# Handing over the next steps' preparation behind both halves of a cell visit, in an mLSTM cell followed by a leaky-ReLU feed-forward

## The chip, the cores and the metric

One core of a Trainium2 chip runs the whole program. The metric is device time in microseconds (us); lower is better. A core has five engines with instruction streams of their own: TensorE (PE, matmuls, its weight loads shown as PEld), VectorE (DVE), ScalarE (ACT), GpSimd (POOL) and SyncE (SP). Nearly all DMAs of this kernel are issued by SP, one after the other.

## The reference

An mLSTM cell runs over 768 time steps for 4 batch entries and 8 heads of 40 values, and its output, laid out as 3072 tokens of 320 values, goes through a feed-forward with 2048 hidden values:

```python
for t in range(S):
    m_new = np.maximum(f_gate[:, :, t] + m, i_gate[:, :, t])
    f_stab = np.exp(f_gate[:, :, t] + m - m_new)
    i_stab = np.exp(i_gate[:, :, t] - m_new)
    m = m_new
    C = f_stab * C + i_stab * np.einsum('bhd,bhe->bhde', vt, kt)
    n = f_stab * n + i_stab * kt
    h_tilde = np.einsum('bhde,bhe->bhd', C, qt)
    denom = np.maximum(np.abs(np.einsum('bhd,bhd->bh', n, qt)[:, :, None]), 1.0)
    y[:, :, t] = sigmoid(o_gate[:, :, t]) * h_tilde / denom
x = y.transpose(0, 2, 1, 3).reshape(B * S, H * D)
h = x @ w_in
out = np.maximum(0.01 * h, h) @ w_out
```

All data are float32 in the profile.

## The kernel before

The sequence is cut into six chunks of 128 tokens. A **step** `s` is one batch entry in one chunk: `s = 4*c + b`, 24 in all. The recurrence is computed in its chunked form: inside a step two halves of 64 tokens are handled with matmuls, and a state `S` is carried from half to half.

**Chunk loop.** For `c` from 1 to 6 the program works through the feed-forward of chunk `c-1` (the list `ffs`, built by `ff_units`) and, between its units, through the cell of chunk `c` (the list `cells`). From `c = 2` on `ffs` has 30 units. Units 0 to 15 are `firsts`: pairs of matmul runs with `w_in` (line 759, tile `ph`, input `xT`), then the leaky ReLU on ACT (line 767) into `acts`. Units 16 to 29 are `fast_units`, the multiplication with `w_out` done with seven products on sums and differences of quarters (Strassen's scheme in Winograd's form), each for `n = 0, 1`: `p1`, `p2`, `p6`, `p7`, `p4`, `p5`, `p3` in this order (matmuls on line 835, tile `po`). The quarter `(n, 0, 1)` of `acts` is read by `p2`, is then overwritten by the difference `s4`, and `s4` is read by `p3`, the last product.

**Cell visits.** `pairs` names the unit behind which cell work is emitted: behind unit 2 `u_parts` for steps 0 and 1 of the chunk, behind unit 6 `u_mix` for both, behind unit 14 `u_parts` for steps 2 and 3, and behind unit 19 (the second `p2`) `u_gates` for the next chunk, then `u_mix` for steps 2 and 3. `u_parts` makes the scores and the first half of the state. `u_mix` multiplies (line 695, tile `pT`), transposes on DVE (`hb`, 702), makes denominators (633 to 635), the gated product `xb` (706), the state sum (596), a POOL product (709), a second DVE transpose into `x` (713), and stores `x` to a scratch `x_dr` in DRAM with four DMAs (716).

**Preparation.** `ahead(s)` prepares step `s`: `prep_kq` on DVE (two transposes, line 505, and two products, line 511), a POOL product for the state (`state_next`, 592), a POOL product for `vu` (478), and ten loads on SP for the step after the next: four of k and four of q (line 398) and two of `ea` (line 421), which wait until `prep_kq` has read the buffers that they overwrite. `u_mix(s)` is followed by `ahead(s + 2)`.

**Gathers.** `gather_x(s)` brings `x_dr[s]` back as `xT`, laid out for `w_in`, with four DMAs (line 730). `xT` has one buffer for a whole chunk, so the gathers start behind unit 15. For the second `u_mix` visit of a chunk (behind unit 19) they follow the visit at once, eight DMAs for two steps. The next chunk's unit 0 reads their result. Behind them come, per step, four loads of the output gate (398), one of k (356), four of v (359) and two broadcasts `w` (413): 22 loads for a visit, called "feed loads" below.

**What sets the order.** PE, DVE, ACT and POOL run in the order in which the program emits (`tc.manual_schedule`). SP is not in that list: its order is made by the framework's planner, which takes the earliest instruction of the program that it holds to be ready. PSUM tiles of the cell share four banks (`psc`), those of the feed-forward four others (`psf`).

Of the kernel before, what the change touches and what calls it, by code (L numbers as in the profile page):

```python
# [13 lines left out]
ALU = mybir.AluOpType  # L14
# [4 lines left out]
def kernel(  # L19
# [26 lines left out]
    nc = tc.nc  # L46
# [44 lines left out]
    def load_fi(c):  # L91
        t = fi[c] = wk.tile([BH, 2, P], F32, name="fi")
        eng = nc.scalar if c < 3 else nc.sync
        eng.dma_start(t[:, 0, :], f_all[:, ts(c, P)])
        eng.dma_start(t[:, 1, :], i_all[:, ts(c, P)])
# [206 lines left out]
    def gates_exp(c):  # L302
        bu, a, na = bus[c]
        if c == 0:
            nc.scalar.activation(bu[:, 1, :], bu[:, 0, :], AF.Exp, bias=a[:BH, P - 1 :], scale=1.0)
            return
        for u in range(2):
            at = ts(u, SL)
            last = SL * (u + 1) - 1
            nc.scalar.activation(bu[:, 2, at], a[:, at], AF.Exp, bias=na[:] if u else 0.0, scale=1.0)  # L310
            nc.scalar.activation(bu[:, 1, at], bu[:, 0, at], AF.Exp, bias=a[:, last : last + 1], scale=1.0)
        if c > 0:
            nc.sync.dma_start(a_dr[c, 0].rearrange("u n t -> n u t"), a[:].rearrange("n (u t) -> n u t", u=2))
            if c > 1:
                nc.sync.dma_start(a_dr[c, 1].rearrange("u n t -> n u t"), bu[:, 2, :].rearrange("n (u t) -> n u t", u=2))
            if 1 < c < NB - 2:
                load_fi(c + 2)
# [498 lines left out]
    def quarter(n, i, k):  # L816

        return acts[:, k * KH : (k + 1) * KH, ts(2 * i + n, P)]
# [5 lines left out]
    def fast_units(g):  # L824


        t1 = low_w[:, :, NH:]
        t2, t3, t4 = t_at
        y = [[None, None], [None, None]]
        t = p1_at  # L830

        def product(n, left, right):
            bank = psf.tile([P, NH], F32, name="po", tag="mm")
            for f in range(KH):
                nc.tensor.matmul(bank[:], lhsT=left[:, f, :], rhs=right[:, f, :], start=f == 0, stop=f == KH - 1)  # L835
            return bank[:]

        def half(n, i, d):
            if y[i][n] is None:
                if i == 0:  # L840
                    y[i][n] = wk.tile([P, Dm], F32, name="y")[:]
                else:
                    y[i][n] = wk.tile([P, H, D1], F32, name="hn")[:].rearrange("p h d -> p (h d)")[:, :Dm]
            return y[i][n][:, ts(d, NH)]

        def send(n, i):
            b = 2 * i + n
            nc.sync.dma_start(out[b * S + g * P : b * S + (g + 1) * P, :], y[i][n])

        def p1(n):  # L850
            got = product(n, quarter(n, 0, 0), low_w[:, :, :NH])
            s1 = quarter(n, 1, 0)
            nc.vector.tensor_tensor(s1, s1, quarter(n, 1, 1), op=ALU.add)
            nc.scalar.copy(t[n], got)
            if n == 1:
                for m in range(2):
                    s2 = quarter(m, 0, 0)
                    nc.vector.tensor_tensor(s2, quarter(m, 1, 0), s2, op=ALU.subtract)

        def p2(n):  # L860
            got = product(n, quarter(n, 0, 1), high_w[:, :, :NH])
            nc.vector.tensor_tensor(half(n, 0, 0), t[n], got, op=ALU.add)
            s4 = quarter(n, 0, 1)
            nc.vector.tensor_tensor(s4, s4, quarter(n, 0, 0), op=ALU.subtract)

        def p6(n):
            got = product(n, quarter(n, 0, 0), t2)
            u2 = half(n, 0, 1)
            nc.scalar.copy(u2, got)
            nc.gpsimd.tensor_tensor(u2, u2, t[n], op=ALU.add)  # L870

        def p7(n):
            got = product(n, s3_at[:, n], t3)
            u3 = half(n, 1, 1)
            nc.scalar.copy(u3, got)
            nc.gpsimd.tensor_tensor(u3, u3, half(n, 0, 1), op=ALU.add)

        def p4(n):
            got = product(n, quarter(n, 1, 1), t4)
            c21 = half(n, 1, 0)  # L880
            nc.scalar.copy(c21, got)
            nc.gpsimd.tensor_tensor(c21, c21, half(n, 1, 1), op=ALU.add)

        def p5(n):
            got = product(n, quarter(n, 1, 0), t1)
            for i in (1, 0):
                nc.vector.tensor_tensor(half(n, i, 1), half(n, i, 1), got, op=ALU.add)  # L887
            send(n, 1)

        def p3(n):  # L890
            got = product(n, quarter(n, 0, 1), high_w[:, :, NH:])
            nc.vector.tensor_tensor(half(n, 0, 1), half(n, 0, 1), got, op=ALU.add)
            send(n, 0)

        return [lambda p=p, n=n: p(n) for p in (p1, p2, p6, p7, p4, p5, p3) for n in range(2)]

    def u_gates(c):
# [43 lines left out]
    def feed(s):  # L941
        load(s)
        spread(s)
# [78 lines left out]
    with tc.manual_schedule(engines={E.PE, E.DVE, E.Activation, E.Pool}):  # L1022
        ffs = first_chunk()
        for s in (B, B + 1):
            feed(s)
            for i in range(1, 3):
                load_late(s, i)
            if s == B:
                load_weights(3)
        for n in range(3):  # L1030
            load_weights(QN + n)
        for s in (B + 2, B + 3):
            feed(s)


        ffs = ffs[2:]
        fetch = {4: (3, 4), 8: (5, 6), 15: (7,)}
        place = (2, 5, 7, 10, 12, 15, 16, 18, 21, 22, 24, 26, 28)
        late = {}
        masks = {0: (2, 3), 12: (4, 5)}  # L1040
        pairs = (2, 2, 6, 6, 14, 14, 19, 19, 19)
        now = (None for n in range(2, QN + NF // 2) for _ in narrow_weights(n))
        for c in range(1, NB + 1):
            if c > 1:
                ffs = ff_units(c - 1)
            cells = cell_units(c) if c < NB else []
            n_ff, n_c = len(ffs), len(cells)
            done = fed = 0
            waiting = []
            for i in range(n_ff):  # L1050
                if c == 1:
                    run(now, 2 if i < 10 else 3 if i < 14 else 4)
                    for n in fetch.get(i, ()):
                        load_weights(QN + n)
                    if i == 0:
                        prep_mask(B)
                        ahead(B)
                        load_fi(3)
                for s, steps in lazy.items():
                    if s in late and late[s] > 0:  # L1060
                        late[s] -= 1
                    else:
                        run(steps, 3)
                for n in masks.get(i, ()) if 1 < c < NB else ():
                    if c * B + n < NS:
                        prep_mask(c * B + n)
                ffs[i]()
                if c + 1 < NB:
                    if i == (1 if c == 1 else 0):
                        gates(c + 1)  # L1070
                    if c == 2 and i == 0:
                        mixed_weights()
                    if i == (3 if c == 1 else 2):
                        gates_exp(c + 1)
                upto = min(n_c, sum(p <= i for p in (place if c == 1 else pairs)))
                while done < upto:
                    fn, s = cells[done]
                    fn(s)
                    done += 1
                    if fn is u_mix:  # L1080
                        waiting.append(s)
                    if fn is u_plain and s < 2 * B - 1 or fn is u_parts and s == 2 * B - 1:
                        ahead(s + 1)
                    elif fn is u_mix:
                        ahead(s + 2)
                    elif fn is u_plain:
                        prep_mask(s + 2)
                        ahead(s + 2)
                if i >= NF - 1:
                    for s in waiting:  # L1090
                        gather_x(s)
                    waiting.clear()
                while fed < done:
                    fn, s = cells[fed]
                    fed += 1
                    if fn in (u_mix, u_plain):
                        load_late(s + NR, 2)
                        if s + NL < NS:
                            feed(s + NL)
# [31 lines left out]
```

## Time and profile before

| | us |
|---|---|
| median of 3 runs | 513.13 (512.97 to 515.71) |
| the profiled execution | 516.18 |
| its span | 514.4 |
| PE busy in it | 496.0 |
| DVE busy | 305.8 |
| ACT busy | 171.3 |
| POOL busy | 130.6 |

The span is what the profile's rows cover; 1.78 us of the profiled execution lie outside it. All starts below are counted from the span's start. Chunks 1 to 5 of the feed-forward start at 140.9, 217.0, 294.7, 371.1 and 446.1 us.

An idle time in brackets at the end of a row stands before the row's first instruction, with what ended it. A row merges several instructions; its time runs from the first start to the last end. SPq is SP's queue of DMA issues.

### The profile page before, as it was taken

What the parts mean: (1) busy time and instruction counts of PE and PEld (TensorE: products, weight loads), DVE (VectorE), ACT (ScalarE), POOL (GpSimd) and SP (SyncE); (2) the same over time, 40 slices, a digit from 0 to 9 for tenths busy, and PEclk for the clock granted to TensorE, in tenths of its full rate; (3) what the DMA queues carried; (4) which work ended last, traced back from release to release, by engine and by line L of the source; (5) the groups of instructions that cost most, each with busy time, mean ns of one, the idle gap of its engine ahead of it and who ended that gap; (6) DMA issues with size and microseconds to landing.
All of it is one profiled execution on the core that took longest, in us unless ns stands there. A gap on an engine that the chain in (4) does not pass through costs nothing.

```text
span 514.4 us, 12486 instructions
## 1 busy us (share of the span) xinstructions
PE 496.0 (96%) x4981; PEld 368.6 (72%) x4981; DVE 305.8 (59%) x515; ACT 171.3 (33%) x478; POOL 130.6 (25%) x175
## 2 busy tenths in 40 slices
PE   8888999999999999999999899999999999999997
PEld 7766878767655589855589855489855589844797
DVE  4769898997965789225789224788224583101411
ACT  3665865550822513022513022513112511022210
POOL 4243353360402305103305103305202103000020
PEclk9867999999999999999999999999999999999999
DMA  9976686888765643567654667654563111200001
GB/s 116 144 208 148 138 215 136 167 193 162 163 146 101 163 96 75 152 116 157 150 123 89 146 123 159 148 120 109 139 127 101 40 52 45 84 1 0 2 1 52
DMA packets 165290, 59.21 MB, mean 115 GB/s; under 512 B 128816, under 2 KB 156016, under 8 KB 165232
## 3 DMA queue, kind: packets, MB, share of 16 engines
q1 hardware_dynamic: 164848, 58.28, 52.3%
q8 instruction: 39, 0.64, 0.6%
q10 hardware_dynamic: 384, 0.13, 0.1%
q14 instruction: 19, 0.16, 0.1%
HBM read 51.68 MB, written 6.70 MB: 113 GB/s over the span
## 4 chain that ended last, share of the span: by engine, by line
PE 67%; SPq 11%; DVE 11%; DMA 5%; issue 3%; ACT 2%; POOL 1%; ACTq 0%; DVEq 0%; POOLq 0%
PE ph L759 37%; PE po L835 21%; SPq L229 4%; PE sd L614 3%; PE po L794 2%; PE pT L695 2%; SPq L354 2%; SPq L398 2%; DMA raw<-in_moe_w_out_dram 1%; DMA S<-in_v_dram 1%; DMA xT<-x_dr 1%; DVE kqT L505 1%; PE sd L619 1%; SPq L730 1%; SPq L368 1%
## 5 line engine op out<-in xcount | busy, mean ns | idle before, releaser
L759 PE MATMUL ph<-xT,w_in 64*128 64x512 f32 (+1 forms) x1120 | 218.6, 538 | 3.4 <-DMA xT<-x_dr 2.3
L759 PEld LDWEIGHTS ph<-xT,w_in 64*128 64x128 f32 x1120 | 110.0, 189 | 97.3 <-issue 86.9
L767 ACT ACTIVATE acts<-ph 128x512 f32<-128x512 f32 (+1 forms) x112 | 54.2, 534 | 192.9 <-PE ph L759 192.8
L835 PEld LDWEIGHTS po<-w_out,acts 128*128 128x128 f32 x640 | 87.3, 190 | 3.8 <-issue 3.8
L835 PE MATMUL po<-w_out,acts 128*128 128x160 f32 x640 | 89.1, 300 | 0.0
L592 POOL TENSOR_TENSOR S<-S,f 40x336 f32<-40x336 f32 x36 | 30.9, 857 | 91.1 <-PE pT L695 64.0
L624 DVE TENSOR_TENSOR qn<-w,sd 64x512 f32<-64x512 f32 x40 | 27.4, 684 | 43.5 <-PE sd L619 23.5
L450 POOL TENSOR_TENSOR w<-w,i 128x512 f32<-128x512 f32 x20 | 28.1, 1411 | 96.3 <-DMA w<-a_dr 87.5
L458 ACT ACTIVATE w<-w,gT 128x64 f32<-128x64 f32 (+1 forms) x192 | 51.5, 349 | 2.7 <-POOL w L450 1.7
L835 PE MATMUL po<-raw,acts 128*128 128x160 f32 x320 | 45.5, 300 | 0.0
L835 PEld LDWEIGHTS po<-raw,acts 128*128 128x128 f32 x320 | 43.9, 190 | 0.3
L794 PE MATMUL po<-w_out,acts 128*128 128x320 f32 x128 | 36.7, 437 | 1.0 <-DVE w_out L263 1.0
L794 PEld LDWEIGHTS po<-w_out,acts 128*128 128x128 f32 x128 | 23.5, 190 | 10.6 <-DVE w_out L263 1.5
L511 DVE TENSOR_TENSOR qn<-kqT,ea 64x512 f32<-64x512 f32 x32 | 28.5, 891 | 0.9
L709 POOL TENSOR_TENSOR xb<-xb,den 128x320 f32<-128x320 f32 x16 | 11.6, 727 | 65.0 <-DVE xb L706 65.0
L702 DVE STREAM_TRANSPOSE hb<-pT 128x512 f32<-128x512 f32 x16 | 11.4, 714 | 28.1 <-PE pT L695 27.8
L887 DVE TENSOR_TENSOR hn<-hn,po 128x160 f32<-128x160 f32 x10 | 3.2, 322 | 40.8 <-PE po L835 25.1
L614 PEld LDWEIGHTS sd<-kqT 40*64 40x64 f32 x640 | 19.9, 135 | 6.1 <-issue 6.1
L822 DVE TENSOR_TENSOR raw<-acts 128x1024 f32<-128x1024 f32 x10 | 11.8, 1222 | 18.3 <-ACT acts L767 18.2
L835 PE MATMUL po<-raw 128*128 128x160 f32 x160 | 22.5, 299 | 0.0
L713 DVE STREAM_TRANSPOSE x<-xb 128x512 f32<-128x512 f32 x16 | 17.9, 1122 | 7.7 <-POOL xb L709 6.9
L835 PEld LDWEIGHTS po<-raw 128*128 128x128 f32 x160 | 22.0, 190 | 0.0
(151 smaller groups left out, 560.1 us busy)
## 6 DMA issues: line engine op xcount, KB each, us to landing
w<-a_dr SPq DMA_DIRECT2D x40, 128.0 KB
rb<-in_k_dram SPq DMA_DIRECT2D x64, 80.0 KB
rb<-in_q_dram SPq DMA_DIRECT2D x64, 80.0 KB
rb<-in_o_gate_dram SPq DMA_DIRECT2D x64, 80.0 KB
ea<-a_dr SPq DMA_DIRECT2D x32, 128.0 KB
kn<-in_k_dram SPq DMA_DIRECT2D x24, 160.0 KB
raw<-in_moe_w_out_dram SPq DMA_DIRECT2D x6, 640.0 KB
S<-in_v_dram SPq DMA_DIRECT2D x80, 40.0 KB
```

The costliest lines, as they stand in the source:

```text
L229: nc.sync.dma_start(to[DP * r : DP * (r + 1), 2 * P * slot : 2 * P * (slot + 1)], src[r, :, SLOTS[r][slot], :],)
L450: nc.gpsimd.tensor_tensor(w, w, cm2.unsqueeze(1).to_broadcast([P, H, SL]), op=ALU.add)
L458: yield nc.scalar.activation(w[:, h, :], w[:, h, :], AF.Exp, bias=gT[c][:, 0, bh : bh + 1], scale=1.0)
L511: nc.vector.tensor_tensor(mixed(s)[rows, 1 - r], d["kqT"][rows, 1].rearrange("p (h t) -> p h t", t=SL), d["ea"][rows], op=ALU.mult,)
L592: nc.gpsimd.tensor_tensor(new, old, g, op=ALU.mult)
L614: nc.tensor.matmul(bank[1 - u][toks, h, :], lhsT=kqT[rows, 0, ts(h, SL)], rhs=kqT[rows, 1, ts(h, SL)], start=True, stop=True,)
L624: nc.vector.tensor_tensor(mixed(s)[toks, u], w[toks], bank[1 - u][toks], op=ALU.mult)
L713: nc.vector.transpose(in_blocks(xq[:]), xb[:].rearrange("p (j n) d -> p j n d", n=TB))
L759: nc.tensor.matmul(ph[r][:, cols], lhsT=w_row(r, slot, j), rhs=xT[DP * r : DP * (r + 1), slot, cols], start=(slot == 0), stop=(slot == KC ...
L767: nc.scalar.activation(acts[:, f, cols], ph[r][:, cols], AF.Prelu, alpha=0.01)
L794: nc.tensor.matmul(po[n][:], lhsT=acts[:, f, ts(n, P)], rhs=w_out[:, f, :], start=(f == 0), stop=(f == NF - 1),)
L835: nc.tensor.matmul(bank[:], lhsT=left[:, f, :], rhs=right[:, f, :], start=f == 0, stop=f == KH - 1)
```

## The change

There are two edits. In `fast_units` the difference `s4` moves from `p2` to `p6`: `p2(0)`, `p2(1)`, `p6(0)`, `p6(1)` are units 18 to 21, and the visit behind unit 19 lies between. In the chunk loop, `ahead(s + 2)` for a `u_mix` is no longer called right after that `u_mix`: it is put on a list and called after the visit's last cell and after the gathers.

```diff
         def p2(n):
             got = product(n, quarter(n, 0, 1), high_w[:, :, :NH])
             nc.vector.tensor_tensor(half(n, 0, 0), t[n], got, op=ALU.add)
-            s4 = quarter(n, 0, 1)
-            nc.vector.tensor_tensor(s4, s4, quarter(n, 0, 0), op=ALU.subtract)
 
         def p6(n):
             got = product(n, quarter(n, 0, 0), t2)
             u2 = half(n, 0, 1)
             nc.scalar.copy(u2, got)
             nc.gpsimd.tensor_tensor(u2, u2, t[n], op=ALU.add)
+            s4 = quarter(n, 0, 1)
+            nc.vector.tensor_tensor(s4, s4, quarter(n, 0, 0), op=ALU.subtract)
...
+                after = []
                 upto = min(n_c, sum(p <= i for p in (place if c == 1 else pairs)))
                 while done < upto:
                     fn, s = cells[done]
...
                     elif fn is u_mix:
-                        ahead(s + 2)
+                        after.append(s + 2)
                     elif fn is u_plain:
                         prep_mask(s + 2)
                         ahead(s + 2)
                 if i >= NF - 1:
                     for s in waiting:
                         gather_x(s)
                     waiting.clear()
+                for s in after:
+                    ahead(s)
                 while fed < done:
```

In the chunk loop only visits with `u_mix` are touched: two for each `c` from 2 to 5. In the second visit of `c = 5`, `ahead` has no step left and does nothing, before and after.

## The prediction

> **What bounds the kernel now.** I read the shares of the chain that ended last first, then that chain in order of time, then PE's own rows at the seams between chunks, then what SP and DVE did just before such a seam.
>
> ```profile
> PE 67%; SPq 11%; DVE 11%; DMA 5%; issue 3%; ACT 2%; POOL 1%; ACTq 0%; DVEq 0%; POOLq 0%
> ```
>
> PE is busy 496.0 of 514.4 us, and the chain is mostly PE. SPq and DVE have a share too; where it lies decides.
>
> ```profile
> 140.98 7.07 PE ph L759 x32
> ...
> 158.89 2.02 PE pT L695 x64
> ...
> 214.26 2.59 DMA xT<-x_dr
> 216.99 8.06 PE ph L759 x32
> ...
> 291.93 2.62 DMA xT<-x_dr
> 294.69 8.02 PE ph L759 x32
> ...
> 371.07 8.17 PE ph L759 x32
> ```
>
> A chunk's first three units are 32 matmul rows. They take 7.07 us in the first of these chunks, where x comes through PE and ACT and not through DRAM, and 8.06, 8.02 and 8.17 in the next three. Twice a gather of x ends right before.
>
> ```profile
> 191.77 1.15 PE L695 MATMUL pT<-qn,S 128*64 128x64 f32 x32
> 193.12 1.15 PE L695 MATMUL pT<-qn,S 128*64 128x64 f32 x32 [0.20 <-DVE f L340]
> 194.20 4.61 PE L835 MATMUL po<-raw,acts 128*128 128x160 f32 x32
> ...
> 216.99 2.95 PE L759 MATMUL ph<-xT,w_in 64*128 64x512 f32 x10 [0.79 <-DMA xT<-x_dr]
> ...
> 294.69 2.87 PE L759 MATMUL ph<-xT,w_in 64*128 64x512 f32 x9 [1.51 <-DMA xT<-x_dr]
> ...
> 371.07 3.49 PE L759 MATMUL ph<-xT,w_in 64*128 64x512 f32 x12 [0.27 <-issue]
> ```
>
> PE stands still before the seams for 0.79, 1.51 and 0.27 us, and the second `pT` of the visit waits for DVE's copy on line 340.
>
> ```profile
> 196.89 1.46 SPq L716 DMA_DIRECT2D x_dr<-x  x4
> 198.45 3.12 SPq L398 DMA_DIRECT2D rb<-in_k_dram  x4
> ...
> 204.88 1.69 SPq L716 DMA_DIRECT2D x_dr<-x  x4
> ...
> 211.66 5.16 SPq L730 DMA_DIRECT2D xT<-x_dr  x8
> ...
> 427.56 5.09 SPq L716 DMA_DIRECT2D x_dr<-x  x8
> 432.82 6.29 SPq L730 DMA_DIRECT2D xT<-x_dr  x8
> ```
>
> From 196.9 to 216.8 SP issues without a break: stores, ten loads, stores, ten loads, and only then the gathers, the last of which goes out at 216.2, after PE has already run dry. The last two rows are the visit of the last cell chunk, where `ahead` has nothing left to do: stores and gathers there stand next to each other, and the chunk that follows, at 446.1, starts with no wait in PE's rows and runs its 160 matmul rows in 34.53 us, even pace throughout. That visit shows what the changed ones should look like.
>
> ```profile
> 191.49 1.22 DVE L864 TENSOR_TENSOR acts<-acts 128x1024 f32<-128x1024 f32 x1
> 192.62 0.22 DVE L338 COPY gT<-tg 128x64 f32<-128x64 f32 x1
> ...
> 196.71 1.26 DVE L505 STREAM_TRANSPOSE kqT<-rb 128x512 f32<-128x512 f32 x2
> ...
> 199.48 0.72 DVE L702 STREAM_TRANSPOSE hb<-pT 128x512 f32<-128x512 f32 x1
> ```
>
> DVE does `s4` ahead of the gate copies, and `prep_kq` of the first step, 196.71 to 199.48, ahead of the second step's `hb`, whose `pT` has been ready since 194.3.
>
> **The change, part by part.** *Second `hb` earlier.* Without `prep_kq` between, the second `hb` starts at 196.7 instead of 199.48, 2.77 us earlier, and the second transpose into x, before at 202.27 to 203.37, ends at 200.6. The first `ahead`'s `state_next` and `vu` on POOL (0.76 and 0.72 us, from 195.80 on) step behind too; the second step's own `state_next` takes their place and POOL is free for line 709 from 196.6, so that product isn't held.
>
> *SP.* The second stores go out at 200.6 instead of 204.88: 4.3 us earlier, because SP no longer has the ten loads (198.45 to 204.8) before them. They take 1.7 us, to 202.3. The gathers stood behind ten more loads (206.66 to 211.6, 5.0 us); now they start at 202.4 instead of 211.66 and take 5.2 us by this visit's row, 6.3 by the row at 432.82, where one of them took 1.67 us instead of 0.61. The last is issued at 206.9 to 208.0 instead of 216.2. A gather lands 2.59 us after its issue (chain, 214.26), so x is complete by 209.5 to 210.6. PE asks for it at about 216.0. Margin: 5.4 to 6.5 us.
>
> *What PE saves at a seam.* Standing still: 0.79 + 1.51 + 0.27 = 2.57 us. First 32 matmul rows: (8.06 - 7.07) + (8.02 - 7.07) + (8.17 - 7.07) = 3.04 us, which no wait row shows: single matmul rows show the two row halves, which run side by side elsewhere, starting one after the other (216.99 and 217.95), since their gathers land one after the other. The 7.07 is confirmed by the chunk at 446.1: 34.53 x 32/160 = 6.91. Together 5.61 us. The bounds: nothing, if something else holds the seam, and 5.61 + 3 x 0.16 = 6.1 if 6.91 is the floor. I take 5.61.
>
> *`s4`.* DVE's copies 338 and 340 come 1.15 us earlier (the step from 191.49 to 192.62), so PE's second `pT` finds its bank free. The two `pT` runs and their gap take 194.20 - 191.77 = 2.43 us, against 2.02 in the visit at 158.89, which has no `u_gates` before it: 0.41 us each, in three chunks (the waits list 0.6 us in three waits of PE on line 340, the rest is the restart): 1.23 us. The waits alone, 0.6 us, are the low end. `s4` itself, 2 x 1.22 us, comes behind the second `prep_kq`, which ends at 206.3, so it ends at about 208.8. `p3(0)` reads it and starts at about 211.7, 3 us later; that is its cover. DVE's sum on line 887, at 209.79, isn't reached. Without cover it would cost at most 2.4 us a chunk.
>
> *`prep_kq` later.* The first one moves from 196.7 to about 200.6; the second ends at 206.3 as before, since DVE does the same work. They serve `u_parts` of the next chunk: 18 us and more of cover. In the visit behind unit 6 they serve `u_parts` behind unit 14: DVE ends them at 251.3, PE starts there at 255.2. This is the tight place. PE comes 2.2 us earlier there in the first chunk and some 5 in the next, while POOL first has to wait for the `w` broadcasts (line 450, second mask 234.92 to 236.19, just ahead of the visit's 236.61). I put the margin at 2 us, then 1; each us beyond is a us of PE, so 0 to 1.5 us of loss, and I take 0.
>
> *The twenty loads behind the gathers.* They go out at 207.6 to 217.6 instead of 198.45 to 211.6. Their readers are the `prep_kq` of the next visit, 235 us and later. The feed loads start at 217.6 to 218.7 instead of 216.93; `w` then lands up to 1.8 us later, which is in the tight place above. SP is the second-busiest: from the stores at 196.89 to those at 273.88 it idles 3.6 us (270.24 to 273.88), and the change adds a hole of some 2.2 us between the two steps' stores.
>
> The Trainium skill has a rule that speaks against this order. "DMA: Bandwidth & Descriptors", section on the anatomy of one DMA, puts most of a fixed 2.0 us on the receipt of the write, longest when the target is HBM, and a gather right behind its stores has to sit that out on SP. The page measured that on GpSimd's path; taken at full, 2 us would be added ahead of each step's gathers, 4 us in all, still inside the margin, and the sum would not change. The rows at 427.56 and 432.82 have this very order: the first gather goes out 0.17 us after the last store, since its own step's stores were 3.6 us old.
>
> *Sum.* 5.61 + 1.23 = 6.84 us. The profiled execution would take 516.18 - 6.84 = 509.34. The median lies 3.05 us below the profiled execution; the same step from it gives 513.13 - 6.84 = **506.3 us**. With the low ends of `s4` and a loss of 1.5 us: 508.4; with 6.1 at the seams and a little more of restart: 505.
>
> **Rivals.** *SP becomes the bound.* SP's cycle is 77.0 us (196.89 to 273.88), 73.4 of it work and waits in the middle; with the 2.2 us hole and one slow gather (1.1 us) 76.7, and PE then wants 77.0 - 2.2 = 74.8 or less. SP falls behind by 2 us a chunk, for three chunks, out of a margin of 5 to 6. If its waits grow and the margin is gone after the first seam, only that seam's gain (0.79 + 0.99 + 0.41 = 2.2) and some 0.3 us in each of two more chunks is kept: 510.3. For it: the last gathers before the stores end only 3.6 us ahead. Against it: several of SP's stops in the cycle are waits for PE, which move with PE.
>
> *The wait at the seam changes its name.* PE could find that `ph` needs a bank or ACT there, or that the seams' waits belong to the profiled execution alone, which is 3.05 us longer than the median. Time: 513.1 or, with `s4`, 512. Against it: the seam at 446.1 has the same banks and products in front of it and no wait.
>
> *Slower: the planner fills SP's holes with loads.* The order of SP is not the program's. At 235.14 to 244.3 it put k, w and v loads of the feed ahead of the x stores that precede them in the code. With the change there are two new holes for that: between the steps' stores, and while the second stores land. Each load put in costs 0.45 to 0.85 us. From about 12 loads the margin is used up; from about 20 the last gather goes out no earlier than today's 216.2. If both steps' 22 feed loads (216.93 to 232.05, 15.1 us) come first, the last gather goes out at 206.9 + 15.1 = 222.0, 5.8 us later than now, in three chunks: 513.13 + 17.4 - 1.2 = 529.3. Against it: a planner fills a hole only while it lasts, and 2.2 us hold about four loads; in the visits behind unit 19 it kept the code's order.
>
> **How the numbers follow.** The forecast, 505 to 508.4, gets 0.62. SP as the bound, 508.4 to 511, 0.16. No gain, 511 to 514, 0.10. SP's order, slower, 0.12. A measurement of this kernel tells a change from none at about 0.5%, that is 510.6 and 515.7. Faster: 0.62 and 0.12 of the second case, 0.74. Same: 0.04 and 0.10, 0.14. Slower: 0.12. The range 505 to 511.5 holds the first two cases and a little of the third, 0.81.
>
> **What would show it.** Right: SP's rows show stores, stores, gathers, loads behind unit 19, with the last gather out 5 us or more before the chunk's first matmul; no PE idle time released by `xT`; first 32 matmul rows of 7.1 us in all chunks; two `pT` runs in 2.0 us after the gates; and `prep_kq` ending before the `u_parts` behind unit 14. Wrong: `w`, `rb` or `kn` loads between stores and gathers; PE waiting on `kqT` in `sd`; POOL's 450 ending after the first `pT` of the visit behind unit 6 by 4 us or more; DVE's `s4` as the releaser of `p3`. The prediction fails most surely if SP's order has changed elsewhere too, since no row here shows that.

## The result, and the profile after

The changed kernel is slower. Its median is 521.5 us (519.35 to 522.66, 4 runs) against 514.04 us before (4 runs on the same chip): a ratio of 1.0138, interval 1.0091 to 1.0184. The forecast was 506.3 us. The profiled execution took 519.35 us, with a span of 517.6. It is the fastest of the four, and the profiled execution of the kernel before (516.18 us) was slower than all four of its runs here: the two traces are 3.2 us apart, the medians 7.5. What the other executions lost beyond the 3.2 us stands in no trace.

The chain that ended last, in order of time (start, us, what), has both the expected gain and its loss in it:

```profile
139.08 7.07 PE ph L759 x32
...
213.87 7.07 PE ph L759 x32
...
268.61 3.93 DMA w<-a_dr
272.70 1.24 POOL w L450
274.02 0.77 POOL S L592
274.86 0.74 POOL xb L709
275.63 1.13 DVE x L713
...
280.52 1.28 DVE kqT L505 x2
...
287.03 1.44 DVE acts L870
288.61 7.13 PE po L835 x32
295.74 7.07 PE ph L759 x32
...
375.34 7.07 PE ph L759 x32
```

Every chunk now starts with 32 matmul rows in 7.07 us, and no gather of x stands in front of one. That part came as forecast. But from 268.6 to 288.6 the chain leaves PE: a `w` broadcast, POOL's mask that waits for it, POOL's and DVE's work of the second visit, and at the end `s4` (line 870 here), which PE waits for. The same happens a chunk later, around 350 to 369.

From one chunk's first `ph` to the next, by these chains:

| chunk of the feed-forward | before, us | after, us |
|---|---|---|
| 1 | 76.0 | 74.8 |
| 2 | 77.7 | 81.9 |
| 3 | 76.4 | 79.6 |
| 4 | 75.1 | 74.0 |

Together 305.2 before and 310.3 after: 5.1 us lost. (The first of these chunks starts 1.9 us earlier in the trace after, which makes it 3.2 us over the whole span.) Chunks 1 and 4 keep their gain; chunks 2 and 3 lose 4.2 and 3.2 us, although each also has the gain in it.

PE's rows of the changed kernel show what the two stalls cost:

```profile
279.91 4.51 PE L835 MATMUL po<-w_out,acts 128*128 128x160 f32 x32
288.61 7.13 PE L835 MATMUL po<-w_out,acts 128*128 128x160 f32 x32 [4.19 <-DVE acts L870]
...
369.25 6.09 PE L835 MATMUL po<-w_out,acts 128*128 128x160 f32 x32 [3.12 <-DVE acts L870]
```

Before `p3` PE is idle for 4.19 and 3.12 us, released by `s4`. The 32 matmul rows after each stall take 7.13 and 6.09 us instead of 4.51. The reason is in the windows view. Each row has a stretch and its length, then busy time and count of PE, PEld, DVE, ACT and POOL, then the granted clock of TensorE (1.00 is full speed), the DMA share and GB/s:

```profile
279.90:284.40 4.50, 4.50 (x34) 4.28 (x32) 4.42 (x7) 0.29 (x1) 4.26 (x6) 1.00 0.23 59
284.40:288.60 4.20, 0.02 (x1) 0.02 (x1) 4.10 (x6) 0.00 (x0) 2.98 (x5) 0.81 0.42 123
288.60:295.70 7.10, 7.09 (x34) 6.93 (x34) 2.33 (x6) 0.00 (x0) 0.00 (x0) 0.63 0.71 169
```

While PE stood still the granted clock fell, and behind the stall it was 0.63 on average. So a stall of 4.19 us costs 4.19 + (7.13 - 4.51) = 6.8 us, the other 3.12 + (6.09 - 4.51) = 4.7 us: 11.5 us against a gain of 6.8. That leaves 4.7 us, near the 5.1 by which the chunk starts moved.

Why is `s4` late? Two SP rows, before and after, tell it. Before, in the visit behind unit 6:

```profile
236.91 2.38 SPq L413 DMA_DIRECT2D w<-a_dr  x4
```

After, in the visit behind unit 6 and the one behind unit 19:

```profile
239.11 5.38 SPq L716 DMA_DIRECT2D x_dr<-x  x8
244.59 1.80 SPq L398 DMA_DIRECT2D rb<-in_k_dram  x4
...
261.30 1.27 SPq L413 DMA_DIRECT2D w<-a_dr  x2
...
267.93 1.28 SPq L413 DMA_DIRECT2D w<-a_dr  x2
269.30 6.14 SPq L730 DMA_DIRECT2D xT<-x_dr  x8
...
276.78 5.37 SPq L716 DMA_DIRECT2D x_dr<-x  x8
282.31 5.22 SPq L730 DMA_DIRECT2D xT<-x_dr  x8
```

Before, the planner had put the k, w and v loads of this visit ahead of its x stores. Now it puts nearly all of them behind the stores and the twenty loads of `ahead`: the four `w` broadcasts go out at 261 to 269 us instead of 237 to 239. POOL's rows, before:

```profile
247.83 2.94 POOL L450 TENSOR_TENSOR w<-w,i 128x512 f32<-128x512 f32 x2
269.58 0.76 POOL L592 TENSOR_TENSOR S<-S,f 40x336 f32<-40x336 f32 x1 [18.80 <-PE pT L695]
```

and after:

```profile
265.59 1.27 POOL L450 TENSOR_TENSOR w<-w,i 128x512 f32<-128x512 f32 x1 [20.11 <-DMA w<-a_dr]
272.67 1.27 POOL L450 TENSOR_TENSOR w<-w,i 128x512 f32<-128x512 f32 x1 [5.80 <-DMA w<-a_dr]
274.02 0.77 POOL L592 TENSOR_TENSOR S<-S,f 40x336 f32<-40x336 f32 x1
```

The masks for the next chunk's first two steps are emitted on POOL before unit 12, well ahead of the second visit. POOL runs in order, so they stand in front of that visit. Nobody needs them before the next chunk, but while they wait for `w`, `state_next` (592) of the second visit waits too: its `pT` was finished at about 266, it starts at 274.0.

DVE carries the delay to PE:

```profile
274.82 0.51 DVE L596 TENSOR_TENSOR S<-S,sd 40x336 f32<-40x336 f32 x1 [6.97 <-POOL S L592]
...
287.03 2.57 DVE L870 TENSOR_TENSOR acts<-acts 128x1024 f32<-128x1024 f32 x2
```

DVE stands for 6.97 us before the state sum, then does both steps' x and both `prep_kq` in order, and only then `s4`, from 287.0 on. PE had asked for it at 284.4.

### The profile page after: what moved, and what is told of

Its sections match the earlier page's. It is cut to its first block, busy times and chain, and to the rows that moved or that the text cites. A ratio compares the mean times of both kernels' runs of the same rounds, so it can differ in the third digit from the quotient of the medians.

```text
span 517.6 us, 12513 instructions
## 1 busy us (share of the span) xinstructions
PE 498.9 (96%) x4981; PEld 373.5 (72%) x4981; DVE 307.9 (59%) x515; ACT 171.9 (33%) x478; POOL 135.0 (26%) x175
## 4 chain that ended last, share of the span: by engine, by line
PE 76%; SPq 9%; DVE 5%; DMA 4%; issue 2%; ACT 2%; POOL 1%; ACTq 0%; POOLq 0%; DVEq 0%
PE ph L759 37%; PE po L835 24%; PE po L794 6%; SPq L229 4%; PE pT L695 3%; PE sd L614 3%; SPq L354 2%; DMA w<-a_dr 1%; SPq L368 1%; DVE kqT L505 1%; PE sd L619 1%; SPq L359 1%; ACT kqT L540 1%; DVE qn L511 1%; PE hN L665 1%
## 5 line engine op out<-in xcount | busy, mean ns | idle before, releaser
L759 PE MATMUL ph<-xT,w_in 64*128 64x512 f32 (+1 forms) x1120 | 214.8, 536 | 1.2 <-ACT acts L767 1.2
L759 PEld LDWEIGHTS ph<-xT,w_in 64*128 64x128 f32 x1120 | 107.5, 189 | 93.9 <-issue 86.6
L835 PE MATMUL po<-w_out,acts 128*128 128x160 f32 x640 | 93.6, 308 | 7.3 <-DVE acts L870 7.3
L835 PEld LDWEIGHTS po<-w_out,acts 128*128 128x128 f32 x640 | 91.4, 197 | 11.5 <-issue 11.5
L794 PEld LDWEIGHTS po<-w_out,acts 128*128 128x128 f32 x128 | 23.6, 190 | 9.3 <-issue 0.3
L596 DVE TENSOR_TENSOR S<-S,sd 40x336 f32<-40x336 f32 x36 | 18.1, 503 | 16.2 <-POOL S L592 15.3
```

The lines of the kernel that those rows point to most:

```text
L596: nc.vector.tensor_tensor(new, new, st[s]["dC", u], op=ALU.add)
L759: nc.tensor.matmul(ph[r][:, cols], lhsT=w_row(r, slot, j), rhs=xT[DP * r : DP * (r + 1), slot, cols], start=(slot == 0), stop=(slot == KC ...
L794: nc.tensor.matmul(po[n][:], lhsT=acts[:, f, ts(n, P)], rhs=w_out[:, f, :], start=(f == 0), stop=(f == NF - 1),)
```

## The experiments

The theories. **A**: late `w` broadcasts hold POOL's masks, these hold the second visit, and `s4` behind that visit on DVE hands the delay to PE. **B**: the deferral behind unit 6 is at fault. **C**: SP is overrun, whatever POOL does. **D**: only the new place of `s4` is wrong. All ratios are to the kernel before, on the same chip.

### e1: s4 alone

Before, with this edit only:

```diff
 def p2(n):
-    s4 = quarter(n, 0, 1)
-    nc.vector.tensor_tensor(s4, s4, quarter(n, 0, 0), op=ALU.subtract)
...
 def p6(n):
+    s4 = quarter(n, 0, 1)
+    nc.vector.tensor_tensor(s4, s4, quarter(n, 0, 0), op=ALU.subtract)
```

> Only s4 moves to p6; ahead stays where it was, so SP's order is that of before. Prediction's step: DVE's gate copies come 1.15 us earlier in three chunks and PE's second pT run finds its bank free, 0.41 us a chunk: 1.2 us less than before, the two pT runs in 2.02 us. s4 ends before p3 asks for it, 3 us of cover. Rival (the s4 move is what made the change slow): p3 waits for s4 here as well, 4 us or more over the chunks, so 3 us or more above before.

Measured: 514.19 against 513.96 us, ratio 0.9997, interval 0.9978 to 1.0015. PE's rows of this kernel:

```profile
190.48 2.08 PE L695 MATMUL pT<-qn,S 128*64 128x64 f32 x64
...
215.43 5.09 PE L759 MATMUL ph<-xT,w_in 64*128 64x512 f32 x20 [0.93 <-DVE il L282]
```

The two `pT` runs are one row without a wait, as forecast, and nothing waits for `s4`. So the place of `s4` doesn't hurt by itself (D's half of the story falls). The 1.2 us do not appear in the median; they lie just outside the interval. SP's row of the gathers shows why:

```profile
210.13 5.18 SPq L730 DMA_DIRECT2D xT<-x_dr  x8
```

The seam still waits for x. PE's row names DVE's `il`, which ended just ahead, but the gathers set the time. Before, PE started 2.73 us after the fifth gather, the first of the second step, was issued (214.26 to 216.99); here it starts 2.69 us after it (212.74 to 215.43). And x comes hardly earlier because PE does: the gathers start 19.65 us after the visit's first `pT`, before 19.89 us. So chunks 1 and 3 take 75.82 and 76.29 us against 76.07 and 76.38 before, 0.25 and 0.09 us less instead of 0.41 each, and the seam takes the rest. Chunk 2 is 1.0 us shorter, but there SP needed 5.2 us for the eight stores of x in the trace of before and 3.5 in this one, so that this can't be put down to `s4`.

### e2 and e6: one visit at a time

The change, with `ahead` deferred only behind unit 19 (e2) or only behind unit 6 (e6, the condition turned round):

```diff
-    after.append(s + 2)
+    if i >= NF - 1:
+        after.append(s + 2)
+    else:
+        ahead(s + 2)
```

> ahead is deferred only in the visits behind unit 19; behind unit 6 it follows each u_mix as before; s4 as in the change. Theory A (POOL's masks wait for w loads that the planner now issues late behind unit 6, since the second visit's new order shifts SP's plan): as slow as the full change, 519 to 523. Theory B (the deferral behind unit 6 is at fault: prep_kq late for u_parts): the gain of the prediction returns, about 507.

> ahead is deferred only behind unit 6, and follows each u_mix behind unit 19 as before; s4 as in the change. SP's order at both visits is that of before apart from the stores standing together. Theory A: the seams still wait for x as in before, POOL's masks are early: 513 to 515, like s4 alone. If the deferral behind unit 6 costs something by itself (prep_kq late for u_parts): above 515, with PE waiting on kqT.

e2: 516.09 us, ratio 1.0039 (1.0022 to 1.0056). SP's and PE's rows of e2:

```profile
258.25 2.42 SPq L413 DMA_DIRECT2D w<-a_dr  x2
...
266.03 1.27 SPq L413 DMA_DIRECT2D w<-a_dr  x2
```

```profile
286.39 6.26 PE L835 MATMUL po<-w_out,acts 128*128 128x160 f32 x32 [2.48 <-DVE acts L870]
...
365.96 6.26 PE L835 MATMUL po<-w_out,acts 128*128 128x160 f32 x32 [2.91 <-DVE acts L870]
```

The same late `w` and the same stall before `p3`, so B falls: deferring behind unit 19 is enough to turn the planner's order behind unit 6. A had expected 519 to 523 us, so its number is missed by 3 us. In the traces the stalls are shorter than in the changed kernel (2.48 and 2.91 us for 4.19 and 3.12): at the first one `w` goes out 2 to 3 us earlier.

e6: 512.69 us, ratio 0.9994 (0.9975 to 1.0013): like s4 alone, as A had it, though 0.3 us under its 513 to 515. Behind unit 6 the stores stand together now, but the k, w and v loads are ahead of them as before. One row of PE at the first seam:

```profile
215.35 6.89 PE L759 MATMUL ph<-xT,w_in 64*128 64x512 f32 x28 [0.95 <-DVE il L282]
```

The wait at the seam is back, and no wait on `kqT` appears in the chunk loop: the deferral behind unit 6 neither gains nor costs.

### e3: masks behind the second visit

The full change, with

```diff
-masks = {0: (2, 3), 12: (4, 5)}
+masks = {0: (2, 3), 20: (4, 5)}
```

> The full change, and the masks of the next chunk's first two steps are emitted on POOL before unit 20 instead of before unit 12, that is behind the second visit. SP's order is the changed kernel's. Theory A: POOL no longer stands before the second visit, the sum over the state and x come in time, PE doesn't wait for s4, the clock stays up, and the prediction's 6.8 us appear: 506 to 509. Theory C (SP is overrun, the stores of x get out late whatever POOL does): x and its gathers stay late, 516 or more.

Measured: 509.43 against 513.96 us, ratio 0.9915 (0.9889 to 0.9941), 0.4 us above the range of A and far from that of C. SP's order is unchanged, `w` still goes out at 261.8 and 268.4. POOL's and PE's rows:

```profile
266.28 0.77 POOL L592 TENSOR_TENSOR S<-S,f 40x336 f32<-40x336 f32 x1 [20.21 <-PE pT L695]
...
276.92 2.94 POOL L450 TENSOR_TENSOR w<-w,i 128x512 f32<-128x512 f32 x2
```

```profile
280.60 8.86 PE L835 MATMUL po<-w_out,acts 128*128 128x160 f32 x64
289.39 7.14 PE L759 MATMUL ph<-xT,w_in 64*128 64x512 f32 x32
```

POOL is free when `pT` ends, the masks come later, and PE goes through `p5` and `p3` into the next chunk without a gap. One number in the code turns 1.4% slower into 0.85% faster. C falls: SP issues the same DMAs in the same order, and keeps up.

### e5: the change without s4

The full change, with `s4` back in `p2` (e1's edit undone).

> The full change with s4 back in p2, ahead of the second visit; ahead stays deferred, and SP's order is the changed kernel's. Theory A (POOL's masks hold the second visit, and s4 behind it on DVE holds p3): the stall before p3 is gone and with it the halved clock; what is left is x, which lands some 25.3 us after the visit's first pT against 24.4 us for PE, so the two later seams wait for the gathers as in before. First seam's gain of 1.8 us kept: 511.5 to 514.5. Theory D (only s4's place is wrong, the rest of the change works): 507.5 to 509.

Measured: 517.53 against 512.73 us, ratio 1.0096 (1.0074 to 1.0119). No theory's number was met. The seam at 291 us has no loss at all: PE no longer has to wait for `s4`, and x just makes it. But the next chunk is hit: PE took 75.2 us for this one, while the `w` broadcasts behind unit 6 go out 82.6 us after the last ones (263.49 and 346.06). The masks now hold the visit behind unit 6 as well: its `state_next` starts at 319.8, 9.6 us after its first `pT` run ended (3.2 us a chunk earlier). PE's and SP's rows of e5:

```profile
346.28 1.15 PE L695 MATMUL pT<-qn,S 128*64 128x64 f32 x32 [1.32 <-DVE f L340]
...
373.39 9.79 PE L759 MATMUL ph<-xT,w_in 64*128 64x512 f32 x32 [4.03 <-DVE y L892]
```

```profile
361.52 6.36 SPq L716 DMA_DIRECT2D x_dr<-x  x8
368.05 5.22 SPq L730 DMA_DIRECT2D xT<-x_dr  x8
```

The masks still hold the second visit (the second one runs at 357.4 to 358.7, while the first `pT` ended at 345.0), the stores go out at 361.5, the last gather at some 372.6, and PE stands for 4.03 us at the seam. The row names a DVE instruction that ended just ahead, but PE starts 2.65 us after the fifth gather was issued (370.74), as at the other seams that wait for x. It loses 2.7 us more in its first 32 rows, during which the clock is halved for 3.4 us. So D falls, and A holds in kind: what is late is the whole visit. `s4` was only the first of its results that PE asked for; with `s4` out of the way it is x.

### e8: only the w broadcasts earlier

The full change, with the `w` broadcasts taken out of the feed and emitted behind `u_parts`:

```diff
     fn, s = cells[fed]
     fed += 1
+    if fn is u_parts and c > 1 and s + NL < NS:
+        spread(s + NL)
     if fn in (u_mix, u_plain):
         load_late(s + NR, 2)
         if s + NL < NS:
-            feed(s + NL)
+            load(s + NL)
+            if fn is u_plain:
+                spread(s + NL)
```

> The full change, s4 in p6 and ahead deferred, with one thing added: the w broadcasts for the step four ahead are emitted behind u_parts, eight and twelve units earlier, instead of with the feed loads; k, v and o of the feed stay where the planner puts them in the changed kernel. Theory A (late w alone, through POOL's masks): no stall before p3, no halved clock, seams without a wait: a ratio of 0.985 to 0.990. If k, v or SP's load as a whole are what holds the second visit: above 1.000.

Measured: 506.89 against 512.81 us, ratio 0.9889 (0.9862 to 0.9916). SP's, POOL's and PE's rows:

```profile
236.84 2.40 SPq L413 DMA_DIRECT2D w<-a_dr  x4
```

```profile
242.41 2.94 POOL L450 TENSOR_TENSOR w<-w,i 128x512 f32<-128x512 f32 x2
264.73 0.76 POOL L592 TENSOR_TENSOR S<-S,f 40x336 f32<-40x336 f32 x1 [19.38 <-PE pT L695]
```

```profile
287.85 7.14 PE L759 MATMUL ph<-xT,w_in 64*128 64x512 f32 x32
```

Four broadcasts go out where they did before the change (the chunk's other four move ahead too, to 264.9), k and v stay late, at 255 to 265, and every stall is gone. That is A's cause by itself.

### e4, e7, e9 and e10: the feed ahead of the deferred calls, and the size of the s4 term

e4 and e9 are the full change with the deferred calls moved behind the feed loads; e7 and e10 are the same with `s4` back in `p2`:

```diff
-                for s in after:
-                    ahead(s)
                 while fed < done:
...
                             feed(s + NL)
+                for s in after:
+                    ahead(s)
```

> The full change, with the deferred ahead calls put behind the feed loads, so that SP issues k, v and w of the step four ahead before the twenty loads of ahead. Theory A: w lands some 10 us earlier than in the changed kernel, POOL's masks are done before the second visit's pT, 506 to 509. Theory C (SP is overrun): the same number of issues in the same chunk, so no gain over the changed kernel, 516 or more.

> The kernel with the feed loads ahead of the deferred ahead calls (e4), with s4 back in p2. There the seams wait for nothing, so the prediction's term for s4 shows alone: the second pT waits for the gate copies again, 0.41 us in three chunks, 1.2 us more than e4: about 508.7. If s4's place is worth nothing: 507.5.

> The kernel of e4 beside e10 on one chip, for the size of the s4 term: 0.986 to 0.990 of before.

> The kernel of e7 beside e9: 1.2 us (0.0024) above e9 by the profile's term for s4; 2.8 us (0.0055) above it if the earlier ratios of e4 and e7 are taken at their word.

Measured: e4 507.47 against 513.96 us, ratio 0.9876 (0.9855 to 0.9898); e7 509.21 against 512.73, 0.9931 (0.9912 to 0.995); then side by side e9 507.42, 0.9892 (0.9865 to 0.9918), and e10 508.29, 0.9917 (0.9886 to 0.9949), both against 512.81. POOL's rows of e4:

```profile
250.89 1.27 POOL L450 TENSOR_TENSOR w<-w,i 128x512 f32<-128x512 f32 x1 [8.22 <-DMA w<-a_dr]
258.12 2.21 POOL L450 TENSOR_TENSOR w<-w,i 128x512 f32<-128x512 f32 x1 [5.96 <-DVE acts L853]
264.89 0.77 POOL L592 TENSOR_TENSOR S<-S,f 40x336 f32<-40x336 f32 x1 [4.56 <-issue]
```

Here the masks still wait for `w`, but they are done at 260.3, before the second visit asks for POOL. That is enough. e4 and e7 ran on different chips, so only their ratios compare: they are 0.0055 apart, 2.8 us. e9 and e10, on one chip, are 0.0025 apart, 1.3 us (0.9 in the medians), and their intervals overlap. From the first chunk's start to the last, single matmul rows give 298.3 us in e4 and e9 and 299.6 in e7 and e10: 1.3 us for `s4`, where the prediction had 1.23. So the medians alone don't settle the size, and the traces do.

Both e8 (506.89) and e4 (507.47) beat the kernel before and the changed one.

## Why the prediction was wrong, point by point

**What the seams are worth: right.** The sum was 5.61 + 1.23 = 6.84 us. In e4 and e9, where nothing else stalls, the five chunk starts span 298.3 us against 305.2 before: 6.9 us. By parts: 5.6 us without the term for `s4` (e7 and e10, 299.6) and 1.3 us for it. The medians fell by 5.4 to 6.5 us in e4, e8 and e9. That the 6.9 us fit so well is in part because both numbers are taken from one trace of before: its chunk 2 took 77.7 us, but 76.7 and 76.2 in e1 and e6, where SP has the same order at that seam and `s4` explains 0.4 us at most. So about 1 us of the sum belongs to that one execution. In the changed kernel itself the first chunk has the whole gain (74.8 us, as in e4).

**The order behind unit 19: right.** SP's order there is stores, stores, gathers, loads, without a load in the holes, and the first of these gathers goes out at 200.97 instead of 211.66 (forecast 202.4). Counted from the visit's first `pT`, which itself comes 1.9 us earlier in this trace, that is 11.1 us where the forecast had 10.6. The 2 us that the prediction would have added ahead of each step's gathers do not show: the first gather goes out 0.17 us after the last store, and the second step's first 0.77 us after the gather before it, where the others are 0.62 to 0.65 us apart.

**The step that failed** is in "the twenty loads behind the gathers": the feed loads were taken to start "at 217.6 to 218.7 instead of 216.93", and `w` to land "up to 1.8 us later", which carries the order of the old trace over to the new kernel. SP's order is made anew when the program is built, and it came out different at a place that the diff hardly touches: the loads of the visit behind unit 6. There `w` went out 24 to 30 us later (four broadcasts from 236.9 to 239.3 before, two from 261.3 and two from 267.9 after). In the sum this is the loss that was taken as 0, with 1.5 us as the most; the two stalls that came of it cost 11.5 us. e2 and e6 show that it is the deferral behind unit 19 that turns this order. Why the planner decides so, no run shows.

**The tight place was the wrong one.** The prediction looked at POOL's masks ahead of the visit behind unit 6. The ones that hurt are emitted before unit 12 and stand ahead of the visit behind unit 19. In the old trace they ran at 247.8 with no wait worth a row, and POOL then idled for 18.8 us, which is why the step looked safe. (In e5 the masks that it looked at are late too, as said there.)

**The price of `s4` without its cover** was put at "at most 2.4 us a chunk", its own duration. What it really carries is the delay of everything that it was put behind: 4.19 and 3.12 us, and then the clock.

**The rivals.** The third, that the planner's order does the harm, named the right agent at the wrong place: no load went between stores and gathers, and its price (529.3) was worked out from gathers. The first, SP as the bound, is refuted by e3: SP's order kept, gain there. The second, that nothing is gained at the seams or only in the profiled execution, falls with the medians of e4, e8 and e9, apart from the 1 us above. The list of what would prove the forecast wrong had it in two places, `s4` as the releaser of `p3`, and an order of SP changed elsewhere.

## What to carry to other kernels

When a change alters the order in which an automatically ordered queue is planned, the old trace says nothing about that queue elsewhere; look at the new order before believing a sum, and ask of every load that can move who stands in front of whom when it is late. An instruction that nobody needs yet, put early on an in-order engine, is harmless only as long as its input comes in time; e3 cured this with one number. And an instruction that has been moved behind a stretch of work inherits that stretch's lateness: price its cover by the stretch, not by itself.

## What the hardware showed unexpectedly

**Short stalls of PE cost clock.** At idle times of 4.19 and 3.12 us in the changed kernel, 2.48 and 2.91 us in e2 and 4.03 us in e5, the granted clock in the records falls to 0.5, for 6.8 us in the first case and 3.4 us in the others, and the matmuls behind run longer (32 rows in 6.1 to 7.1 us for 4.51 in the changed kernel and e2). In the kernel before, the waits at the seams, 0.79 and 1.51 us, left it at 1.00. The Trainium skill, "TensorE: Matmul & The Clock Gate", in the section on what is actually happening with the clock gate, has PE fall to half clock after an idle window of about 3.4 us. The size of the step and the length of the half-clock stretch agree; but 2.48 us of idle were enough here, so a stall that is shorter than the page's window can't be counted as free of it.

The fall can also come when PE is at work again: at the first stall of e2 and in e5 it comes 1.06 and 1.17 us after PE has resumed. In the 3.41 us before the five falls PE was busy for 0.50 to 1.17 us, so PE need not have been idle throughout. And the longest single stall does not decide alone: in the start of e3 the clock falls at 76.65 us, with no idle time above 0.94 us just before, where PE was busy for 1.78 of the last 3.41 us with small matmuls.
